# A transform and MLP kernel: first batch from rows in natural order, copies within SBUF, weight chunks interleaved with the first steps

## The chip, the cores and the metric

One core of one Trainium2 chip. The time is device microseconds of one execution; medians of several runs are given. A profile shows the clock as 1.00 wherever the trace has no record of it; there the spacing of the matmul passes has to be read instead. Ratios are the mean time of one kernel's runs over that of the other's of the same rounds, so not quite the ratio of the medians that are quoted.

## The reference

A 2-D Fourier transform (real part) over 8 batches of 3008 x 256, and on its result an MLP with a sigmoid-approximated GELU, 256 to 2048 to 256. The two weights reach the core as 64-bit floats.

```python
X = np.fft.fft(x, axis=1)              # x: (8, 3008, 256)
X = np.fft.fft(X, axis=2)
y = X.real.astype(np.float32).reshape(24064, 256)
h = y @ w_in                           # (256, 2048)
g = h * (1.0 / (1.0 + np.exp(-1.702 * h)))
out = (g @ w_out).astype(np.float32)   # (2048, 256)
```

## The kernel before

The transform over 3008 = 94 x 32 rows is done in two stages. Stage 1 needs row m together with the row that mirrors it, so x is copied once in reversed order through DRAM (`turn`), loaded beside itself, folded in place on VectorE and GpSimd (`fold1`), and multiplied (`mix1`). A spill to DRAM and a fill from it (`spill`, `fill`) turn the result to the layout of stage 2. The last transform, over 256, is folded into w_in (`fold_w`). SBUF is the core's on-chip memory; PSUM is the small one beside it into which TensorE writes its sums. The main loop has 384 steps, 48 a batch; one step makes 256 hidden columns twice (`hidden`), a GELU, four sums of the fast product (`sums`) and 28 matmul passes into the output (`product`). `pa` and `pb` are the results of `hidden`, `psa` those of `nyquist_weights`, four columns for each chunk of w_in.

Both weights come in four chunks each, and each chunk is rounded from 64 to 32 bits: a square on ScalarE and a clamp on GpSimd (`bounds`), five operations on VectorE and an integer add on GpSimd (`rounded`).

```python
def rounded(out, key):
    ...
    dve.scalar_tensor_tensor(m[:], g[:], LOW * LOW, m[:], op0=ALU.is_ge, op1=ALU.mult)
    dve.tensor_scalar(r, lo, scalar1=28, scalar2=1, ...)
    dve.tensor_scalar(a[:], bits, ...)
    dve.scalar_tensor_tensor(a[:], bits, 0xC0000000, a[:], ...)
    dve.scalar_tensor_tensor(a[:], lo, 29, a[:], ...)
    nc.gpsimd.tensor_tensor(out.bitcast(U32), a[:], r, op=ALU.add)
def sums(t):                                # per step
    nc.gpsimd.tensor_tensor(s1, a21, a22, op=ALU.add)
    nc.gpsimd.tensor_tensor(s3, a11, a21, op=ALU.subtract)
    nc.vector.tensor_tensor(s2, s1, a11, op=ALU.subtract)
    nc.vector.tensor_tensor(s4, a12, s2, op=ALU.subtract)
# order of the start (cut)
turn(0, 17, 32); load_x(0, ...); ...; round_in(0)
for c in range(NCH):
    fold1(0, c, ...); mix1(0, c)
load_in(3, nc.sync); spill(0); fill(0); fold_w(0)
for n in range(1, NCK):                     # all of w_in before step 0
    round_in(n); ...; fold_w(n)
nyquist_weights(); round_out(0); ...
rotate(0); stage2(0, 0, 0); stage2(0, 0, 1); nyquist(0, 0)
for i in range(1, NCK):                     # w_out in steps 0, 2, 4
    at(2 * i - 2, round_out, i)
```

## Time and profile before

The marks that matter are the end of stage 1 of the first batch, the start of step 0 (its first `pa` pass), and the start of step 7, from which TensorE works with hardly a gap.

| before | us |
|---|---|
| median of 3 runs | 2132.07 |
| end of stage 1, batch 0 | 47.2 |
| step 0 starts | 86.7 |
| step 7 starts | 149.6 |
| steps 0 to 7 | 62.9 |

Read the marks from the timeline: the first line that writes `pa` is step 0, and each further group of four `pa` passes is one step more. These are the lines of step 0 and step 7 (start, duration, engine, line):

```profile
86.72 2.07 PE L304 MATMUL pa<-pq,wcs 128*128 128x256 f32 x4
...
149.57 1.03 PE L304 MATMUL pa<-pq,wcs 128*128 128x256 f32 x4
```

### The profile page before, as it was taken

Reading aid. Unit: us, or ns where it says so; the run is one execution under the profiler, and the core shown is the slowest. Engines: PE = TensorE matmul, PEld = TensorE weight load, DVE = VectorE, ACT = ScalarE, POOL = GpSimd, SP = SyncE. Lnnn points to the kernel's source line nnn. Section 1 sums busy time; section 2 is a strip of 40 time slices with the busy share of each in tenths; the row PEclk is TensorE's granted clock in tenths of the full one; section 3 lists DMA queues with packets and bytes.
Section 4 is the critical chain, followed back from the end, with each engine's and each line's share of the span. In section 5 each row is a group of like instructions: output and inputs, shape, how many; then the busy total and the mean of one; then the engine's idle time right before and its main releaser. Section 6 shows DMA issues by size and latency. Waiting matters only on the chain.

```text
span 2130.6 us, 36175 instructions
## 1 busy us (share of the span) xinstructions
PE 2030.1 (95%) x14594; PEld 1907.7 (90%) x14594; DVE 1427.3 (67%) x2713; ACT 674.1 (32%) x947; POOL 772.0 (36%) x1061
## 2 busy tenths in 40 slices
PE   4579999999999999999999999999999999999998
PEld 2379999999999999998999899999999999999997
DVE  4466666766676667666666766676666667667666
ACT  1223333333333333333333333333333333333332
POOL 3445322353224522254223432244322542222222
PEclk9779999999999999999999999999999999999999
DMA  7701151123321034211421124121332112101100
GB/s 213 204 20 6 50 112 6 47 25 65 78 40 19 20 65 81 50 6 50 84 35 47 18 42 109 6 49 23 65 79 25 6 45 50 17 20 11 20 21 20
DMA packets 44098, 103.87 MB, mean 49 GB/s; under 512 B 4770, under 2 KB 29090, under 8 KB 41566
## 3 DMA queue, kind: packets, MB, share of 16 engines
q1 hardware_dynamic: 42848, 97.29, 24.4%
q10 hardware_dynamic: 1084, 4.29, 0.6%
q8 instruction: 114, 1.87, 0.4%
q14 instruction: 52, 0.43, 0.1%
HBM read 58.31 MB, written 48.78 MB: 50 GB/s over the span
## 4 chain that ended last, share of the span: by engine, by line
PE 41%; DVE 38%; issue 11%; ACT 7%; DMA 2%; POOL 1%; ACTq 0%; DVEq 0%; SPq 0%; POOLq 0%
PE po L351 24%; DVE dif L316 8%; DVE h L311 7%; DVE h L318 7%; PE pa L304 6%; DVE s L335 6%; PE pb L304 6%; DVE s L336 6%; ACT v L310 5%; PE ps L179 2%; DVE u L374 1%; PE ps L208 1%; DVE os L374 1%; ACT xt L185 1%; DMA Xr<-in_x_dram 1%
## 5 line engine op out<-in xcount | busy, mean ns | idle before, releaser
L323 ACT ACTIVATE h<-h 128x1024 f32<-128x1024 f32 x384 | 405.9, 1057 | 1370.1 <-DVE h L318 1346.2
L333 POOL TENSOR_TENSOR s<-h 128x256 f32<-128x256 f32 x384 | 279.8, 729 | 1260.3 <-issue 931.1
L351 PE MATMUL po<-wt,s 128*128 128x128 f32 x4608 | 650.3, 278 | 25.7 <-DVE s L335 25.7
L311 DVE TENSOR_TENSOR h<-v,pb 128x512 f32<-128x512 f32 x384 | 264.0, 687 | 607.5 <-ACT v L310 581.0
L351 PEld LDWEIGHTS po<-wt,s 128*128 128x128 f32 x4608 | 585.9, 194 | 26.5 <-DVE s L335 26.5
L351 PE MATMUL po<-wo,h 128*128 128x128 f32 x3072 | 474.4, 277 | 24.7 <-DVE u L374 23.5
L351 PEld LDWEIGHTS po<-wo,h 128*128 128x128 f32 x3072 | 433.5, 193 | 56.9 <-DVE u L374 38.7
L304 PE MATMUL pa<-pq,wcs 128*128 128x256 f32 x1536 | 397.5, 381 | 0.0
L304 PE MATMUL pb<-pq,wcs 128*128 128x256 f32 x1536 | 395.1, 380 | 0.0
L316 DVE SCALAR_TENSOR_TENSOR dif<-nb,af,pb 128x256 f32<-128x256 f32 x768 | 332.0, 473 | 0.0
L304 PEld LDWEIGHTS pb<-pq,wcs 128*128 128x128 f32 x1536 | 292.4, 190 | 40.0
L304 PEld LDWEIGHTS pa<-pq,wcs 128*128 128x128 f32 x1536 | 267.3, 192 | 25.2 <-issue 1.5
L318 DVE TENSOR_TENSOR h<-v,dif 128x512 f32<-128x512 f32 x384 | 275.0, 716 | 13.2
L334 POOL TENSOR_TENSOR s<-h 128x256 f32<-128x256 f32 x384 | 280.1, 729 | 0.0
L335 DVE TENSOR_TENSOR s<-s,h 128x256 f32<-128x256 f32 x384 | 247.5, 645 | 20.8 <-POOL s L333 20.8
L351 PE MATMUL po<-wo,s 128*128 128x128 f32 x1536 | 236.4, 277 | 0.0
L351 PE MATMUL po<-wt,h 128*128 128x128 f32 x1536 | 235.7, 276 | 0.0
L310 ACT COPY v<-pa 128x512 f32<-128x512 f32 x384 | 219.6, 572 | 2.6 <-PE pa L304 2.6
L336 DVE TENSOR_TENSOR s<-h,s 128x256 f32<-128x256 f32 x384 | 202.6, 528 | 13.1
L351 PEld LDWEIGHTS po<-wo,s 128*128 128x128 f32 x1536 | 204.6, 194 | 0.0
L351 PEld LDWEIGHTS po<-wt,h 128*128 128x128 f32 x1536 | 203.9, 193 | 0.0
L167 POOL TENSOR_TENSOR xt<-xt 94x510 f32<-94x510 f32 (+1 forms) x59 | 78.3, 1327 | 4.6
(57 smaller groups left out, 715.7 us busy)
## 6 DMA issues: line engine op xcount, KB each, us to landing
out_dram<-os SPq DMA_DIRECT2D x176, 128.0 KB
Td<-xt SPq DMA_DIRECT2D x8, 1536.0 KB
t<-Td SPq DMA_DIRECT2D x8, 1536.0 KB
Xr<-in_x_dram SPq DMA_DIRECT2D x8, 1410.0 KB
xt<-in_x_dram SPq DMA_DIRECT2D x7, 1280.0 KB
xt<-Xr SPq DMA_DIRECT2D x7, 1200.0 KB
nb<-pq SPq DMA_DIRECT2D x23, 256.0 KB
raw<-in_moe_w_out_dram SPq DMA_DIRECT2D x4, 1024.0 KB
```

The lines of the kernel that those rows point to most:

```text
L167: eng.tensor_tensor(low, low, free(t, up + D - 1, [-D, n], [-1, D - 1]), op=ALU.add)
L304: nc.tensor.matmul(ps[:, i * 256:(i + 1) * 256], lhsT=wcs[cs][:, f * 128:(f + 1) * 128], rhs=pq[:, cs, ks], start=True, stop=True)
L310: nc.scalar.copy(v[:], pa[:])
L311: nc.vector.tensor_tensor(h[:, 0].rearrange("p f k -> p (f k)"), v[:], pb[:], op=ALU.add)
L316: nc.vector.scalar_tensor_tensor(dif[:, c], nb[:, ks], af2[:, f:f + 1], pb[:, c], op0=ALU.mult, op1=ALU.subtract)
L318: nc.vector.tensor_tensor(free(h[:], 512 + NB - 1, [NB, 16], [-1, NB]), v[:].rearrange("p (a k) -> p a k", k=NB), dif[:].rearrange("p (a k ...
L323: nc.scalar.activation(ht[t][:], ht[t][:], ACTF.Gelu_apprx_sigmoid)
L333: nc.gpsimd.tensor_tensor(s1, a21, a22, op=ALU.add)
L334: nc.gpsimd.tensor_tensor(s3, a11, a21, op=ALU.subtract)
L335: nc.vector.tensor_tensor(s2, s1, a11, op=ALU.subtract)
L336: nc.vector.tensor_tensor(s4, a12, s2, op=ALU.subtract)
L351: nc.tensor.matmul(pot[n][:, i, q, :], lhsT=lhs[:, q * 128:(q + 1) * 128], rhs=rhs, start=(p == 0 and i == 0 and q == 0), stop=(p == NP - ...
```

## The change

Its intent is to start the main loop earlier. The first batch is no longer reversed: stage 1 takes rows in natural order with extra matrices (`w1x`) for the mirrored rows, so x is loaded straight in four chunks, at the price of twice the matmuls. Its result is moved to the layout of stage 2 by twelve copies within SBUF. Only the first chunk of w_in and of w_out is made before step 0; the others are spread over steps 0 to 5, and GpSimd's last part of a rounding (`finish_...`) is put behind the next step's sums.

```diff
+    def mix_first(c): ...
+                nc.tensor.matmul(ps[...], lhsT=w1[:, l0, :], rhs=el[:, q, c0:c1], start=True, stop=False)
+                nc.tensor.matmul(ps[...], lhsT=upper, rhs=eu[:, 3 - q, c0:c1], start=False, stop=True)
+    def shuffle_first():
+        t4 = t4t[0] = tp.tile([128, NG, D], F32, tag="t4", name="t4")
+        for a in range(NG):
+            nc.sync.dma_start(out=t4[:, a, :], in_=xt[0][8 * a:8 * a + 8, 0:16, :])
...
-        nc.gpsimd.tensor_tensor(out.bitcast(U32), a[:], r, op=ALU.add)
+        return lambda: nc.gpsimd.tensor_tensor(out.bitcast(U32), a[:], bits, op=ALU.add)
...
-    turn(0, 17, 32)
-    load_x(0, [(0, 8), (8, 16)])
+    load_first()
...
+    shuffle_first()
     bounds(("in", 0))
     bounds(("in", 1))
     round_in(0)
+    finish_in(0)
+    load_in(2, nc.sync)
+    fold_w(0)
...
+    at(0, round_in, 2)
+    at(1, fold_w, 1)
+    at(1, finish_in, 2)
+    at(1, round_out, 1)
+    at(2, finish_out, 1)
+    at(2, round_in, 3)
+    at(3, fold_w, 2)
...                       # (cut: loads, bounds, rotate, chunks 2 and 3)
```

More of the change, by code (lines that the diff above doesn't have):

```diff
@@ L33 @@
 NW = 19
+NX = 15
 PIECES = (0, 80), (80, 94)
@@ L57, in tables @@
     cos, sin = np.cos(angle), np.sin(angle)
-    w1 = np.zeros((NA, NW, NG * NU, 2))
+    w1 = np.zeros((NA, NW + NX, NG * NU, 2))
     w1[:, 1:16, :, 0], w1[:, 1:16, :, 1] = cos[:, 1:16], sin[:, 1:16]
@@ L61, in tables @@
     w1[:, 17, :, 0], w1[:, 18, :, 1] = sin[:, 0], sin[:, 16]
+    w1[:, NW:, :, 0], w1[:, NW:, :, 1] = cos[:, :16:-1], -sin[:, :16:-1]
     j, k2 = np.arange(16)[:, None], np.arange(NB)[None, :]
@@ L81, in tables @@
     small = [t.reshape(128, -1) for t in (m2, rot, cd)]
-    return w1.reshape(NA, NW, 96).astype(np.float32), np.concatenate(small, 1).astype(np.float32)
+    return w1.reshape(NA, NW + NX, 96).astype(np.float32), np.concatenate(small, 1).astype(np.float32)
 @with_exitstack
@@ L185, in mix1, with load_first, fold_first, mix_first @@
         nc.scalar.copy(full[:, 2 * c:2 * c + 2, :].rearrange("p j d -> p (j d)"), ps[0:96, :])
+    e4 = {}
+    def load_first():
+        t = xt[0] = xp.tile([96, NB, D], F32, tag="x", name="xt")
+        src = x[0].rearrange("(p j) d -> p j d", j=NB)
+        for c in range(4):
+            for lo, hi in (((0, 4), (29, 32), (16, 17)), ((4, 8), (25, 29)), ((8, 12), (21, 25)), ((12, 16), (17, 21)))[c]:
+                for p0, p1 in PIECES:
+                    nc.sync.dma_start(out=t[p0:p1, lo:hi, :], in_=src[p0:p1, lo:hi, :])
+    def fold_first(c):
+        t = xt[0]
+        el, eu = (hp.tile([NA, 4, D], F32, tag="h", name=n) for n in ("el", "eu"))
+        e4[c] = el, eu
+        first = 29 - 4 * c
+        runs = [(el, 0, 4 * c, 4, False)]
+        runs += [(eu, 0, first, 4, True)] if c else [(eu, 0, first, 3, True), (eu, 3, 16, 1, False)]
+        for e, i, lo, n, flip in runs:
+            fwd, rev = free(t[0:NA], lo * D + 1, [D, n], [1, H - 1]), free(t[0:NA], lo * D + D - 1, [D, n], [-1, H - 1])
+            nc.gpsimd.tensor_copy(free(e[:], i * D, [D, n], [H, 2]), free(t[0:NA], lo * D, [D, n], [H, 2]))
+            nc.vector.tensor_tensor(e[:, i:i + n, 1:H], fwd, rev, op=ALU.add)
+            nc.vector.tensor_tensor(e[:, i:i + n, H + 1:D], *((rev, fwd) if flip else (fwd, rev)), op=ALU.subtract)
+    def mix_first(c):
+        ps = bank("ps1")
+        el, eu = e4[c // 2]
+        for i in range(2):
+            jj, o = 2 * c + i, i * D
+            q = jj % 4
+            ends = ((0, 16, 0, H + 1), (17, 18, H + 1, D)) if jj == 0 else ((jj, NW + jj - 1, 0, D),)
+            for l0, l1, c0, c1 in ends:
+                upper = w1[:, l1, :] if l1 < NW else w1x[:, l1 - NW, :]
+                nc.tensor.matmul(ps[0:96, o + c0:o + c1], lhsT=w1[:, l0, :], rhs=el[:, q, c0:c1], start=True, stop=False)
+                nc.tensor.matmul(ps[0:96, o + c0:o + c1], lhsT=upper, rhs=eu[:, 3 - q, c0:c1], start=False, stop=True)
+        nc.scalar.copy(xt[0][:, 2 * c:2 * c + 2, :].rearrange("p j d -> p (j d)"), ps[0:96, :])
+    def shuffle_first():
+        t4 = t4t[0] = tp.tile([128, NG, D], F32, tag="t4", name="t4")
+        for a in range(NG):
+            nc.sync.dma_start(out=t4[:, a, :], in_=xt[0][8 * a:8 * a + 8, 0:16, :])
     def spill(b):
@@ L193, in fill, with rotate @@
         nc.sync.dma_start(out=t4[:], in_=Td[b].rearrange("(a p) d -> p a d", p=128))
-    def rotate(b):
-        col = t4t[b][:, :, H]
+    def rotate(b, a0=0, a1=NG, copy=None):
+        col = t4t[b][:, a0:a1, H]
         ps = bank("psr")
-        nc.tensor.matmul(ps[:, 0:NG], lhsT=rot, rhs=col, start=True, stop=True)
-        nc.vector.tensor_copy(col, ps[:, 0:NG])
+        nc.tensor.matmul(ps[:, 0:a1 - a0], lhsT=rot, rhs=col, start=True, stop=True)
+        (copy or nc.vector.tensor_copy)(col, ps[:, 0:a1 - a0])
     def stage2(b, blk, cs):
@@ L252, in rounded @@
         a = cv.tile([128, 1024], U32, tag="a", name="a")
-        r = g[:].bitcast(U32)
         dve = nc.vector
         dve.scalar_tensor_tensor(m[:], g[:], LOW * LOW, m[:], op0=ALU.is_ge, op1=ALU.mult)
-        dve.tensor_scalar(r, lo, scalar1=28, scalar2=1, op0=ALU.logical_shift_right, op1=ALU.bitwise_and)
         dve.tensor_scalar(a[:], bits, scalar1=3, scalar2=0x3FFFFFF8, op0=ALU.logical_shift_left, op1=ALU.bitwise_and)
@@ L260, in rounded, with finish_in, finish_out @@
         dve.scalar_tensor_tensor(a[:], lo, 29, a[:], op0=ALU.logical_shift_right, op1=ALU.bitwise_or)
-        nc.gpsimd.tensor_tensor(out.bitcast(U32), a[:], r, op=ALU.add)
+        dve.tensor_scalar(bits, lo, scalar1=28, scalar2=1, op0=ALU.logical_shift_right, op1=ALU.bitwise_and)
+        return lambda: nc.gpsimd.tensor_tensor(out.bitcast(U32), a[:], bits, op=ALU.add)
     wst = {}
+    last = {}
     def round_in(n):
         wst[n] = hp.tile([128, 2, 512], F32, tag="h", name="wst")
-        rounded(wst[n][:].rearrange("p i f -> p (i f)"), ("in", n))
+        last["in", n] = rounded(wst[n][:].rearrange("p i f -> p (i f)"), ("in", n))
     def round_out(n):
         ps = slice(2 * n, 2 * n + 2)
-        rounded(wo[:, ps].rearrange("p f q n -> p (f q n)"), ("out", n))
+        last["out", n] = rounded(wo[:, ps].rearrange("p f q n -> p (f q n)"), ("out", n))
+    def finish_in(n):
+        last["in", n]()
+    def finish_out(n):
+        ps = slice(2 * n, 2 * n + 2)
+        last["out", n]()
         b11, b12, b21, b22 = (wo[:, ps, q, :] for q in range(4))
@@ L282, in fold_w, with nyquist_weights @@
             nc.scalar.copy(wcs[cs][:, n * 512:(n + 1) * 512], ps[:])
-    def nyquist_weights():
+    def nyquist_weights(n):
         ps = bank("psa")
-        for f in range(NF):
+        for f in range(4 * n, 4 * n + 4):
             nc.tensor.matmul(ps[:, f:f + 1], lhsT=wcs[1][0:1, f * 128:(f + 1) * 128], rhs=ones[:, 0:1],
                              start=True, stop=True)
-        nc.vector.tensor_scalar(af2[:], ps[:, 0:NF], scalar1=2.0, scalar2=None, op0=ALU.mult)
+        nc.scalar.activation(af2[:, 4 * n:4 * n + 4], ps[:, 4 * n:4 * n + 4], ACTF.Copy, scale=2.0)
     NP = NF // 2
@@ L390 @@
     NCK = DF // 512
-    turn(0, 17, 32)
-    load_x(0, [(0, 8), (8, 16)])
+    assert NCK == 4
+    w1x = tp.tile([128, NG, D], F32, tag="t4", name="w1x")[0:NA].rearrange("p a d -> p (a d)")[:, 0:NX * 96]
+    w1x = w1x.rearrange("p (j n) -> p j n", j=NX)
+    for p0, p1 in PIECES:
+        nc.scalar.dma_start(out=w1[p0:p1], in_=tab1[p0:p1, 0:NW])
+    for p0, p1 in PIECES:
+        nc.scalar.dma_start(out=w1x[p0:p1], in_=tab1[p0:p1, NW:])
+    load_first()
+    load_in(0, nc.scalar)
     nc.scalar.dma_start(out=small[:], in_=tab2)
-    load_in(0, nc.scalar)
-    for p0, p1 in PIECES:
-        nc.scalar.dma_start(out=w1[p0:p1], in_=tab1[p0:p1])
+    load_in(1, nc.scalar)
+    load_out(0, nc.scalar)
     nc.vector.memset(ones[:], 1.0)
-    for n in range(1, 3):
-        load_in(n, nc.scalar)
+    for c in range(4):
+        fold_first(c)
+        if c:
+            mix_first(2 * c - 2)
+            mix_first(2 * c - 1)
+    mix_first(6)
+    mix_first(7)
+    shuffle_first()
     bounds(("in", 0))
@@ L402 @@
     round_in(0)
-    for c in range(NCH):
-        fold1(0, c, nc.gpsimd if c in (1, 4, 6) else nc.vector)
-        mix1(0, c)
-    load_in(3, nc.sync)
-    spill(0)
-    fill(0)
-    fold_w(0)
-    bounds(("in", 2))
-    for n in range(1, NCK):
-        round_in(n)
-        load_out(n - 1, nc.sync)
-        bounds(("in", n + 2) if n + 2 < NCK else ("out", n + 2 - NCK))
-        fold_w(n)
-    nyquist_weights()
-    round_out(0)
-    load_out(3, nc.sync)
-    if B > 1:
-        turn(1, 17, 32)
-        load_x(1)
-    rotate(0)
+    finish_in(0)
+    load_in(2, nc.sync)
+    fold_w(0)
+    bounds(("out", 0))
+    round_in(1)
+    finish_in(1)
+    load_out(1, nc.sync)
+    nyquist_weights(0)
+    bounds(("in", 2))
+    round_out(0)
+    finish_out(0)
+    load_in(3, nc.sync)
+    rotate(0, 0, 4, nc.scalar.copy)
     for cs in range(2):
@@ L432 @@
     n = len(steps)
-    for i in range(1, NCK):
-        at(2 * i - 2, round_out, i)
-        if i + 1 < NCK:
-            at(2 * i - 2, bounds, ("out", i + 1))
+    at(0, round_in, 2)
+    at(0, load_out, 2, nc.sync)
+    at(0, bounds, ("out", 1))
+    at(1, fold_w, 1)
+    at(1, nyquist_weights, 1)
+    at(1, rotate, 0, 4, NG)
+    at(1, finish_in, 2)
+    at(1, round_out, 1)
+    at(1, load_out, 3, nc.sync)
+    at(1, bounds, ("in", 3))
+    if B > 1:
+        at(1, turn, 1, 17, 32)
+        at(1, load_x, 1)
+    at(2, finish_out, 1)
+    at(2, round_in, 3)
+    at(2, bounds, ("out", 2))
+    at(3, fold_w, 2)
+    at(3, nyquist_weights, 2)
+    at(3, finish_in, 3)
+    at(3, round_out, 2)
+    at(3, bounds, ("out", 3))
+    at(4, finish_out, 2)
+    at(4, round_out, 3)
+    at(5, fold_w, 3)
+    at(5, nyquist_weights, 3)
+    at(5, finish_out, 3)
     for b in range(B):
```

## The prediction

> **What bounds the kernel now.** I read the page's slices first. TensorE is at nine tenths or more from the fourth slice on (a slice is 53 us); only the first three are thin, and that is the part this change touches.
>
> ```profile
> PE   4579999999999999999999999999999999999998
> ...
> PEclk9779999999999999999999999999999999999999
> ```
>
> Then the timeline, to find where TensorE becomes the bound. The loop's steps are counted by their four `pa` passes. Step 0 begins at 86.72 us, step 7 at 149.57 us. From step 7 on one step follows another without a wait, 0.87 + 0.86 + 3.12 = 4.85 us each for the hidden pieces and the product. Whatever lies behind step 7's start is TensorE-bound and the same in both kernels, so its 2130.6 - 149.6 = 1981.0 us are taken as fixed, and the prediction is one question: when does step 7 start in the changed kernel?
>
> Third, the chain of waits over the first 160 us (start, duration, what):
>
> ```profile
> 0.74 18.29 DMA Xr<-in_x_dram
> ...
> 21.12 8.46 DMA xt<-Xr
> ...
> 41.83 5.40 PE ps L179 x12
> 47.23 4.91 PE psw L281 x8
> ...
> 55.47 9.50 DMA raw<-in_moe_w_out_dram
> ...
> 69.28 3.70 PE psw L281 x8
> 72.98 3.67 PE psa L287 x32
> ...
> 86.79 2.00 PE pa L304 x4
> ...
> 97.88 2.39 POOL wo L261
> 100.27 0.07 issue
> 100.33 0.73 POOL wt L275
> ```
>
> The reader is to see three stages: 29.6 us in which x is reversed through DRAM and loaded, about 18 us of first-stage matmuls, about 40 us in which all four chunks of w_in are rounded and folded one after another, and then steps 0 to 6 at 19.9 us for two steps (92.73 to 112.65 to 132.57 us, the starts of the rounding of w_out), because GpSimd finishes a whole chunk (2.39 + four times 0.73 + 1.06 us) before it may make the sums of the step.
>
> Last, the first-stage matmul by itself, first 60 us and then 150 us to the end (durations are minimum/median/maximum):
>
> ```profile
> L179 PE MATMUL ps<-xt,w x30: 631/634/743, 31.8 to 46.6; 94*96 94x256 f32 x30
> ...
> L179 PE MATMUL ps<-xt,w x210: 377/378/420, 160.2 to 1749.2; 94*96 94x256 f32 x105
> ```
>
> and the same stage beside the next one on TensorE:
>
> ```profile
> 37.99 9.24 PE L179 MATMUL ps<-xt,w 94*96 94x256 f32 x20 [1.20 <-DVE xt L170]
> 47.02 8.53 PE L281 MATMUL psw<-wst,small 128*128 128x512 f32 x16
> ```
>
> In the first batch a pass of 256 columns is spaced at about 0.43 us; later four passes take 0.87 us, 0.22 each. In all of its 15 us the first stage never reached the faster rate; the 128x128 fold passes after it went from 0.86 to 0.43 us at 50.2 us.
>
> **What the Trainium skill says.** "TensorE: Matmul & The Clock Gate", section "What's actually happening": two clock states, half rate when idle and full rate after about 3.4 us of sustained work. The trace has the two rates (634 against 378 ns), and full-size passes warm within 3.2 to 6 us here, but the 94x96 passes of 37.99 to 47.23 us stayed at the slow rate for over 9 us. Trace and page differ; I follow the trace. "DMA: Bandwidth & Descriptors", section "Two DMAs through the same engine are not ordered": a DMA that reads what another wrote must wait for its semaphore. The trace agrees: the fill through Td is issued at 55.00 us, 7.1 us after the spill at 47.92 us. Same page, "How many engines (k)" in the section on the semaphore's 16: the slowest dimension of both sides decides, so the new 8-partition copies would run on eight engines. No run here shows that yet.
>
> **The change part by part.**
>
> Removed: the DRAM reversal of batch 0, its in-place folding (26.96 to 44.1 us on VectorE and GpSimd), the spill and fill of batch 0, and the wait of step 0 for all four w_in chunks, 16 `psa` columns and the first w_out chunk.
>
> Added, loads. x comes in four chunks of about 0.77 MB on one queue, on the other w1 0.69 MB, w1x 0.54 MB, raw in 1.05 MB, small 0.46 MB, and two more raw chunks. The windows of before show 386 to 414 GB/s between 12 and 18 us. At an estimated 390 GB/s from 2 us on, split over two queues, chunk 0 and the weights are there by about 7 us, chunks 1, 2, 3 at about 11, 15 and 19 us. VectorE's fold is four operations of 508 columns a chunk; 510 columns took 0.69 us, so 2.8 us a chunk, 11 us in all, ready at about 7.7, 13, 17.5 and 24 us (chunks 2 and 3 also wait for buffers that the matmuls of chunks 0 and 1 free).
>
> Added, matmuls. Each pair of rows now takes four matmuls of 256 columns or their equal (before two, except for the end rows), two passes each: 8 x 8 = 64 such passes in place of 34 (the end rows counted by width). At 0.43 us they are 27.5 us, at 0.22 us 14 us. Starting at 7.7 to 9 us they end at M = 35 to 36.5 us if they stay slow: TensorE is then behind the loads at every chunk. If they warm up, the last chunk's arrival leads and M is 25 to 28 us.
>
> From M to step 0, on the path: last copy 0.65 us; then ScalarE's square, which now stands behind the eight copies, 1.1; five VectorE operations (1.26 + 0.69 + 1.26 + 1.26 + 0.69, 5.2 us as at 8.83 to 13.90 us); GpSimd add 2.4: M + 9.5. Four fold matmuls, cold again, 6.0 us as at 62.34 us: copies done M + 16.3. Four `psa` columns about 0.9, two more squares and small copies on ScalarE before the `rotate` copy: M + 18.9. Two stage-2 blocks, copies and the row broadcast: step 0 at about M + 21.6. The shuffle (12 copies of 128 KB) starts at M + 0.7, and its first four groups are needed only at M + 17, so I count it as hidden.
>
> From step 0 to step 7, the same durations walked in order on each engine: step 0's h ends at M + 25.7; round in 2 at 30.9; step 1's h at 34.2; then VectorE idles until 38.0 for the second `rotate`, which stands behind fold 1 and its copies on ScalarE; then four times a rounding of 5.15 us and a step of 3.3 us (0.69 + 2 x 0.43 + 0.69 + 0.65 + 0.43): h of step 5 at M + 73.6. Fold 3, its copies and `psa` lead to step 6 at M + 76.9, its hidden and product 4.9 us to step 7 at M + 81.7. The steps 0 to 7 thus take 60 us against 63 us before: GpSimd's long finish no longer stands before the sums, but the three w_in chunks have moved in. The gain is almost all in step 0: about 57 us in place of 86.7.
>
> Sum with M = 36: step 7 at 117.7 us in place of 149.6, 31.9 us less; span 2098.7, and the measured time lies 1.5 us over the span, so 2100. With M = 26: 2090.
>
> **Rivals.** (1) The doubled matmuls warm up. For it: the page, and they are back to back where before's had gaps. Against it: 9 us of nearly gapless passes without it. It would take 8 to 11 us more off: 2089 to 2092. I give it one in four. (2) The shuffle or the late weights become the wait. Eight source partitions feed each copy; if twelve took over 16 us, step 0 would slip by the excess. For the late chunks the load waits for a raw buffer: w_in 2 is issued at M + 7.5 and needed at M + 17; spare 5 us. It would cost 0 to 8 us: to 2108. (3) Batch 1's x is now loaded late: its reversal is issued only after the last w_out chunk, at about M + 43 us. Before, reversal to issue of the next load took 9.4 us (82.39 to 91.78), the load after it 8.5 us, so it lands by M + 65, and is needed in step 7. If it slips, step 8's fold waits and a few us are given back. (4) VectorE runs without the 3 to 4 us idle pieces that my order of copies gives: 4 us less.
>
> **Range and chances.** Three quarters at about 2100 with a spread of 5, one quarter at about 2090: 2098, eight times in ten within 2087 to 2108. Two per cent is 42.6 us or 2089.4; only the warm case with nothing lost elsewhere passes it, 0.17. Slower by 2% would need every part to fail: 0.01.
>
> **What would show it.** Right: step 0 at 55 to 59 us and step 7 at 115 to 120 us; the first-stage passes at a median near 634 ns from 8 to 36 us; TensorE idle for about 9 us after them; VectorE without waits over 2 us between steps 2 and 5; 4.85 us steps after step 7. Wrong: first-stage passes at 378 ns, M below 30 us, or a wait for the shuffle or for batch 1's x, or a stretch behind step 7 that isn't 1981 us.

## More of the kernel before

One line more is needed later: VectorE's first sum during the weight stage, from the listing of that source line between 60 and 155 us (durations are minimum/median/maximum in ns).

```profile
L335 DVE TENSOR_TENSOR s<-s,h x7: 655/664/929, 105.0 to 153.8; 128x256 f32<-128x256 f32 x7
```

The reader is to see that this operation takes about 0.66 us here.

## The result, and the profile after

The changed kernel takes 2134.35 us (median of 4 runs, 2132.13 to 2135.22) against 2131.74 us of before in the same rounds: ratio 1.0011, 95% interval 0.9994 to 1.0028. It is the same. The profiled run has a span of 2130.3 us; it is the fastest of the four (2132.13 us).

| mark, us | before | predicted | after |
|---|---|---|---|
| end of stage 1, batch 0 | 47.2 | 36 | 41.1 |
| step 0 starts | 86.7 | 57.6 | 73.0 |
| steps 0 to 7 | 62.9 | 60.1 | 80.3 |
| step 7 starts | 149.6 | 117.7 | 153.3 |
| from step 7 to the end of the span | 1981.0 | 1981.0 | 1977.0 |

The lines of step 0 and step 7 in the changed kernel:

```profile
72.97 2.08 PE L356 MATMUL pa<-pq,wcs 128*128 128x256 f32 x4
...
153.26 1.03 PE L356 MATMUL pa<-pq,wcs 128*128 128x256 f32 x4
```

So the loop does start 13.7 us earlier, and then the same seven steps take 17.4 us longer. The slices of the page show both: the first two are a tenth fuller than before (5 and 6 for 4 and 5), the third is a tenth emptier (6 for 7), and from the fourth on they are full as before.

```profile
PE   5669999999999999999999999999999999999998
...
PEclk9789999999999999999999999999999999999999
```

The chain of waits of the changed kernel over the first 165 us (start, duration, what) shows where the time goes. L230 is a copy within SBUF, L387 VectorE's first sum, L375 the GELU.

```profile
41.71 0.77 SPq L230
...
56.89 1.73 SPq L230
...
58.80 8.12 DMA raw<-in_moe_w_in_dram
...
70.97 2.07 PE psn L265 x2
73.04 2.00 PE pa L356 x4
...
85.64 2.19 DVE s L387
...
90.65 1.06 ACT h L375
91.71 0.97 ACT wcs L334 x2
92.67 0.04 issue
92.72 1.86 PE psa L339 x8
```

The reader is to see two things. First, issuing the twelve copies lasts from 41.7 to 58.6 us; the load of w_in chunk 2 stands behind them in the same queue, is issued at 58.8 us and read only from 67 us on, and step 0 stands behind that: not because it needs chunk 2, but because in ScalarE's order the square of chunk 2 (`bounds`) stands before the copy of `rotate`, which stage 2 of the first block waits for. Second, in the steps the chain runs over VectorE (its roundings, and first sums of up to 2.19 us) and over GELU, weight copies and `psa` in turn. What the sums meet is seen in the timeline (start, duration, engine, line; these are lines of step 5):

```profile
136.88 0.68 DVE L363 TENSOR_TENSOR h<-v,pb 128x512 f32<-128x512 f32 x1
137.04 2.36 POOL L305 TENSOR_TENSOR wo<-a,m 128x1024 uint32<-128x1024 uint32 x1 [3.02 <-DVE m L304]
137.48 2.21 DVE L387 TENSOR_TENSOR s<-s,h 128x256 f32<-128x256 f32 x1
```

VectorE's sum starts 0.44 us after GpSimd's finishing add and ends 0.3 us after it. While GpSimd works, it stands. The operation just before it, which takes one of its inputs from PSUM, keeps its 0.68 us. It started first, but the same operation of step 4 (126.91 us) runs wholly inside another finishing add (125.26 to 127.63 us) and takes 0.69 us: it is not held. The same listing as shown for before, 60 to 155 us, gives for the changed kernel:

```profile
L387 DVE TENSOR_TENSOR s<-s,h x6: 419/2213/2258, 85.6 to 150.8; 128x256 f32<-128x256 f32 x6
```

The median is 2.2 us where it was 0.66. The Trainium skill has the rule that I did not look up: "SBUF — State Buffer", section "SBUF: two separate sides", says that VectorE with two SBUF inputs and a GpSimd operation that reads SBUF share a pair of ports, that whichever starts first holds it for its whole instruction, and that the other waits. The trace agrees, as these lines show.

How much this is can be added up from one window of the steps, first before, then changed (its start and end and its length, then the busy time of TensorE's matmuls and weight loads, VectorE, ScalarE and GpSimd with the number of instructions, then clock, share of the DMA engines and GB/s):

```profile
86.72:149.57 62.85, 38.24 (x198) 35.46 (x197) 34.65 (x51) 13.76 (x17) 26.59 (x30) 0.72 0.36 95
```
```profile
72.97:153.26 80.29, 53.18 (x248) 42.63 (x247) 60.86 (x66) 19.56 (x28) 42.09 (x34) 0.75 0.37 101
```

In the changed kernel VectorE is busy for 60.9 us. Its work there is five roundings of 5.05 us (1.22 + 0.69 + 1.23 + 1.22 + 0.69), seven times 2.25 us for h (0.69 + 0.87 + 0.69), six times 0.85 us of sums (0.42 + 0.43) and 0.17 us: 46.3 us with every duration as it is when nothing else runs. Some 14.6 us are standing still inside an instruction, which the busy time hides. About half of it is in four of the six first sums; the rest is in second sums, roundings (the third operation takes 1.63 us in place of 1.23 each time) and h. In before's window, three roundings and what of h and the sums falls into it make 34.0 us so, and VectorE is busy for 34.7 us: hardly any excess, because there GpSimd's finish always stood between VectorE's work and never beside it.

The first stage has such a block too, on the last fold of x beside GpSimd's two clamps:

```profile
31.76 2.90 DVE L212 TENSOR_TENSOR eu<-xt 94x508 f32<-94x508 f32 x1
...
31.94 2.17 POOL L290 TENSOR_SCALAR m<-raw 128x1024 f32<-128x1024 f32 x2
```

The other operations of this kind there take 0.68 us; here TensorE waits 0.58 us for it.

The copies within SBUF, by windows of 2 us (first two of the first load stage, then one amid the copies, then one of a weight load alone; the last three numbers are the granted clock, the mean busy share of the 16 DMA engines and GB/s):

```profile
8.00:10.00 2.00, 0.74 (x2) 0.40 (x2) 1.04 (x2) 0.00 (x0) 0.49 (x1) 1.00 0.97 221
10.00:12.00 2.00, 0.00 (x0) 0.00 (x0) 0.33 (x1) 0.00 (x0) 0.30 (x1) 1.00 0.98 224
...
52.00:54.00 2.00, 2.00 (x4) 0.68 (x3) 1.99 (x1) 0.00 (x0) 0.91 (x1) 1.00 0.40 97
...
68.00:70.00 2.00, 1.78 (x8) 1.78 (x8) 0.00 (x0) 0.65 (x3) 2.00 (x2) 0.50 1.02 412
```

The copies move 97 GB/s and leave more than half of the engines idle (0.40), which fits the eight engines that the prediction took from the Trainium skill ("DMA: Bandwidth & Descriptors"). And the first loads move 221 to 224 GB/s with all engines busy, where a weight load alone reaches 412. This is how the first fold waits, and TensorE for it:

```profile
11.67 0.55 DVE L211 TENSOR_TENSOR eu<-xt 94x381 f32<-94x381 f32 x1 [2.63 <-DMA xt<-in_x_dram]
...
13.04 0.72 PE L224 MATMUL ps<-eu,w 94*96 94x129 f32 x2 [3.74 <-DVE eu L211]
```

In the trace the loads of the start share eight semaphores, so that from the ninth issue on (7.29 us) each waits until an earlier load has landed. But the two transfers that the first of these lines needs were issued at 1.69 and 2.05 us, without such a wait, and landed only at 10.8 and 11.6 us. The waiting of issues did not hold the first fold; the slow transfers did.

### The profile page after: what moved, and what is told of

It is laid out like the page before. It is cut to its first block, busy times and chain, and to the rows that moved or that the text cites. A ratio compares the mean times of both kernels' runs of the same rounds, so it can differ in the third digit from the quotient of the medians.

```text
span 2130.3 us, 36302 instructions
## 1 busy us (share of the span) xinstructions
PE 2039.4 (96%) x14626; PEld 1912.7 (90%) x14626; DVE 1438.3 (68%) x2707; ACT 673.6 (32%) x952; POOL 774.7 (36%) x1058
## 4 chain that ended last, share of the span: by engine, by line
DVE 43%; PE 33%; issue 12%; ACT 9%; DMA 2%; SPq 1%; ACTq 0%; DVEq 0%; POOL 0%
PE po L403 19%; DVE dif L368 10%; DVE h L363 8%; DVE h L370 8%; DVE s L387 7%; DVE s L388 7%; ACT v L362 6%; PE pa L356 5%; PE pb L356 5%; DVE u L426 1%; PE ps L181 1%; DVE os L426 1%; ACT xt L187 1%; PE ps L253 1%; ACT pq L255 1%
## 5 line engine op out<-in xcount | busy, mean ns | idle before, releaser
L375 ACT ACTIVATE h<-h 128x1024 f32<-128x1024 f32 x384 | 405.9, 1057 | 1369.6 <-DVE h L370 1345.4
L387 DVE TENSOR_TENSOR s<-s,h 128x256 f32<-128x256 f32 x384 | 250.8, 653 | 2.0 <-POOL s L385 2.0
L169 POOL TENSOR_TENSOR xt<-xt 94x510 f32<-94x510 f32 (+1 forms) x56 | 73.8, 1318 | 4.4
```

The costliest lines, as they stand in the source:

```text
L169: eng.tensor_tensor(low, low, free(t, up + D - 1, [-D, n], [-1, D - 1]), op=ALU.add)
L375: nc.scalar.activation(ht[t][:], ht[t][:], ACTF.Gelu_apprx_sigmoid)
```

## The experiments

My theory after the result: the expected gain went three ways, (a) the copies hold back a load that step 0 needs, (b) in the steps VectorE and GpSimd block each other and ScalarE's order makes VectorE wait, (c) stage 1 ends 5 us late because its loads are slow. The main rival: the interleaving is harmless, and the new first batch with its late loads is what slows everything behind it. Thirteen kernels ran, in rounds of three against before; "after" stands for the changed kernel.

| run | median us | ratio to before | step 0 | steps 0 to 7 | step 7 |
|---|---|---|---|---|---|
| after | 2134.35 | 1.0011 | 73.0 | 80.3 | 153.3 |
| e1_oldw | 2136.90 | 1.0034 | 93.4 | 60.4 | 153.8 |
| e2_oldx | 2126.64 | 0.9979 | 68.7 | 78.9 | 147.7 |
| e3_dram | 2123.69 | 0.9962 | 63.5 | 80.6 | 144.1 |
| e4_early | 2124.07 | 0.9962 | 62.8 | 80.6 | 143.5 |
| e5_noadd | 2123.65 | 0.9967 | 73.7 | 69.7 | 143.3 |
| e6_warm | 2133.96 | 1.0011 | 74.2 | 81.3 | 155.6 |
| e7_fold | 2122.60 | 0.9961 | 74.3 | 69.7 | 144.0 |
| e8_both | 2115.29 | 0.9925 | 64.4 | 68.7 | 133.0 |
| e9_all3 | 2105.82 | 0.9874 | 65.4 | 59.6 | 125.1 |
| e10_early | 2114.01 | 0.9916 | 58.4 | 75.4 | 133.8 |
| e11_pitch | 2133.97 | 1.0006 | 72.9 | 81.4 | 154.3 |
| e12_ports | 2132.09 | 1.0001 | 71.7 | 80.1 | 151.8 |
| e13_early_noadd | 2102.27 | 0.9861 | 56.0 | 67.2 | 123.2 |

The half-widths of the 95% intervals are about 0.0015 to 0.0018. No ratio differs from 1 by 2%; what is read here are smaller differences that lie outside the intervals, and the marks in the traces. Not all runs were taken in the same rounds.

**e1_oldw**: the new first batch alone.

```diff
+    for n in range(1, NCK):
+        round_in(n); finish_in(n); ...; fold_w(n)      # before step 0, as in the kernel before
-    at(0, round_in, 2) ... at(5, finish_out, 3)
+    at(2 * i - 2, round_out, i); at(2 * i - 2, finish_out, i)
```

> Only the new first batch; all weights rounded and folded before step 0, as in the kernel before. If the interleaved weights give the gain back, this is faster than the changed kernel: first stage ends near 41 us as there, then about 40 us of weights and 63 us of steps 0 to 7 as before, so step 7 near 144 us and about 2127 us. If the new first batch is itself what gives it back, step 7 stays at 150 us or later and the time at 2132 us or more.

Measured: 2136.90 us, neither of the two in full. The steps take 60.4 us, so without interleaving they are as short as before; that half held. But step 0 comes at 93.4 us and not near 81: its chain of waits goes through the same twelve copies, issued from 41.7 to 58.8 us, and through a w_in load behind them that is landed at 67.7 us. The copies hurt this order more, since here step 0 does need all four chunks of w_in and the last of them stands behind the copies. The new first batch alone makes step 0 6.7 us later than before (93.4 against 86.7). Against the changed kernel, interleaving brought step 0 forward by 20.4 us and lengthened the steps by 19.9 us.

**e2_oldx**: the interleaved weights alone, first batch as before.

```diff
-    load_first(); ... fold_first(c); mix_first(...); shuffle_first()
+    turn(0, 17, 32); load_x(0, ...); fold1(0, c, ...); mix1(0, c); spill(0); fill(0)
```

> Only the interleaved weights; first batch by the reversal through DRAM as before. If the interleaved steps are slow by themselves (80 us from step 0 to step 7, as in the changed kernel), step 0 comes near 65 us and step 7 near 145 us: about 2128 us. If the slow steps come from the new first batch and its late loads, steps 0 to 7 take 60 to 63 us: about 2110 us.

Measured: 2126.64 us, steps 78.9 us. The interleaved steps are slow without the new first batch and its loads. The main rival falls. And step 0 comes at 68.7 us, 4.3 us earlier than with the new first batch: with the copies in front of the load, the new first batch lost time at step 0.

**e3_dram** and **e4_early**: the copies replaced by a spill and fill; and the w_in load issued after four of the copies.

```diff
-    shuffle_first()
+    spill(0)                    # e3_dram
+    fill(0)
```
```diff
-    shuffle_first()
+    shuffle_first(0, 4)         # e4_early
     ...
     load_in(2, nc.sync)
+    shuffle_first(4, NG)
```

> The changed kernel with the twelve copies within SBUF replaced by one spill and one fill through DRAM. If the copies hold up the load of w_in chunk 2, that load lands near 56 instead of 67 us, step 0 comes about 10 us earlier (63 us) and the time is about 2122 us. If step 0 waits for something else (bandwidth, ScalarE's order), it stays within 2 us of 73 us and the time at 2132 us.

> The changed kernel with the load of w_in chunk 2 issued after four of the twelve copies. If only its place in the queue behind the copies costs, step 0 comes near 63 us and the time near 2122 us, as with the copies through DRAM. If the copies slow the load by sharing the DMA engines, it lands late all the same and step 0 gains under 4 us.

Measured: step 0 at 63.5 and 62.8 us, 2123.69 and 2124.07 us: both as expected. The issue line and the square that reads the load, in e4's timeline:

```profile
47.63 0.64 SPq L275 DMA_DIRECT2D raw<-in_moe_w_in_dram  x1
...
58.67 1.17 ACT L291 ACTIVATE g<-raw 128x1024 f32<-128x1024 f32 x1
```

Nothing waits in front of the second line any more. The place in the queue was the cost, 10 us, and not the copies' own landing or the shared engines: in e4 eight of the twelve are still under way when step 0's path runs. Against e2 (68.7 us) the new first batch now does bring step 0 forward, by 5 to 6 us. Part (a) is shown.

**e5_noadd**: GpSimd's finishing adds taken away; the results are truncated, a tiny error made on purpose (the result still counts as correct).

```diff
-        dve.scalar_tensor_tensor(a[:], lo, 29, a[:], ...)
+        dve.scalar_tensor_tensor(out.bitcast(U32), lo, 29, a[:], ...)
-        return lambda: nc.gpsimd.tensor_tensor(out.bitcast(U32), a[:], bits, op=ALU.add)
+        return lambda: None
```

> The changed kernel without GpSimd's eight finishing adds: the last VectorE operation of a rounding writes the result, so it is truncated and not rounded to nearest (a deliberate, tiny error). If VectorE's two-input operations stand still while GpSimd works, the sums that took 2.2 us fall to about 0.65 us, steps 0 to 7 shrink from 80 to 66 to 70 us and the time to about 2118 us (some 2 to 4 us of it from the shorter chain ahead of step 0). If the order of ScalarE's work sets the steps, the sums get shorter but the steps hardly, and the time is about 2128 us.

Measured: 2123.65 us, steps 69.7 us. The sum's listing, 60 to 155 us:

```profile
L387 DVE TENSOR_TENSOR s<-s,h x8: 410/435/954, 86.1 to 151.0; 128x256 f32<-128x256 f32 x8
```

From 2.21 to 0.44 us: the add was what it stood for. The steps shrank by 10.6 us as the first theory has it. The 2 to 4 us ahead of step 0 did not come, since step 0 waits for the load there. The run alone cannot part the collisions from the shorter chain of a rounding; the traces do. Between step 0 and step 7 VectorE's busy time fell from 60.9 to 51.2 us, with the same work, while its waits there hardly changed (14.1 and 13.5 us): what went was the standing still. Some 5 us over its 46.3 us of work remain, beside GpSimd's clamps and its own sums.

**e7_fold**: the fold of a w_in chunk one step earlier in the order.

```diff
-    at(1, fold_w, 1)
-    at(1, nyquist_weights, 1)
+    at(0, fold_w, 1)            # and chunk 2 at 2 in place of 3, chunk 3 at 4 in place of 5
+    at(0, nyquist_weights, 1)
```

> The changed kernel with the fold of w_in chunks 1, 2, 3 one step earlier in the order (after steps 0, 2, 4 in place of 1, 3, 5), so that its copies on ScalarE no longer wait for the next step's GELU. If the chain GELU, copies, psa, hidden, VectorE sets the steps, VectorE's idle pieces of 4.6, 1.7 and 7.9 us go, steps 0 to 7 take about 66 us and the time is about 2118 us. If VectorE against GpSimd is what sets them, at most 4 us come off: 2128 us or more.

Measured: 2122.60 us, steps 69.7 us. VectorE's waits between step 0 and step 7 (us in total, times, longest), first in the changed kernel, then in e7:

```profile
DVE h L363 <- PE pb L356: 22.8, 3, 13.3
DVE t L245 <- PE psr L244: 4.6, 1, 4.6
```
```profile
DVE h L363 <- PE pb L356: 18.2, 4, 13.9
```

The longest is the one before step 0. Without it 14.1 us became 4.3 us, and the steps lost 10.6 us; VectorE's busy time stayed (60.9 and 60.2 us). So ScalarE's order costs as much as the collisions, and this, too, I had expected a little larger (14 us).

**e6_warm**: five full-size matmuls on constants in the middle of stage 1.

```diff
+        if c == 2:
+            for i in range(5):
+                nc.tensor.matmul(ps[:], lhsT=dummy[:, 0:128], rhs=dummy[:], ...)
```

> The changed kernel with five full-size 128x512 matmuls on constant data between the first-stage matmuls of chunks 0 and 1. If the clock, once it is up, stays up under 94x96 passes, the passes after them fall from 634 to 378 ns, the first stage ends near 38 us (then bound by the arrival of the last chunk) and the time falls by about 3 us. If the shape itself keeps or brings the slow rate, the passes stay at 634 ns, the first stage ends near 47 us and the time rises by about 6 us.

Measured: 2133.96 us. The clock rose about 1 us into those 5 us (the first full-size pass is spaced at 0.85 us, the second at 0.53, the others at 0.43) and stayed up under the 94x96 passes that followed:

```profile
18.62 1.06 PE L224 MATMUL ps<-eu,w1x 94*96 94x256 f32 x2
19.47 4.98 PE L463 MATMUL warm<-dummy 128*128 128x512 f32 x10
24.29 0.60 PE L223 MATMUL ps<-el,w 94*96 94x256 f32 x2
...
31.20 0.59 PE L223 MATMUL ps<-el,w 94*96 94x256 f32 x2
36.19 1.14 PE L224 MATMUL ps<-eu,w1x 94*96 94x256 f32 x2 [4.39 <-DVE eu L212]
```

Two passes take 0.60 us where they took 1.06, until TensorE waits 4.4 us for the last chunk and is slow again. The end of stage 1 did not move to 38 us but to 42.4: with a fast TensorE the last chunk's load and fold are the bound, and the rest then ran at the slow rate. About 2 us of the 4.4 are again VectorE's last fold beside GpSimd's clamps, 2.88 us in place of 0.68. Inconclusive for the time, clear for the clock.

**e8_both** (e4 and e7) and **e9_all3** (e4, e5 and e7): the edits are those shown.

> Both repairs: w_in chunk 2 loaded after four copies, and the folds one step earlier. If the two waits are separate, the gains add: step 0 near 63 us, steps 0 to 7 near 66 us, about 2110 us. If the earlier step 0 only moves the wait into the late w_out loads, the steps stay at 80 us and the time at about 2123 us.

> Both repairs and also no finishing adds on GpSimd (results truncated, a deliberate tiny error). With VectorE's collisions and ScalarE's order both gone the prediction's own walk should hold: steps 0 to 7 in 58 to 62 us, time near 2107 us. If the steps stay at 66 us or more, a third cause is in them.

Measured: e8 2115.29 us; by the marks both gains are there in full (step 0 at 64.4, steps 68.7 us), though 5 us above the 2110 hoped for, since e7's own share had been put at 14 us and was 10.6. e9 2105.82 us, steps 59.6 us. With the finishing adds and the order gone, the steps take what the prediction's walk said, 60.1 us. That the two agree so closely is in part luck: the walk has the adds, which e9 lacks, and in e9 VectorE is still busy for 51.0 us, some 5 us more than its work, which the walk lacks. No third cause of size is needed for the steps. Part (b) is shown.

**e10_early** and **e13_early_noadd**: e8 with the squares of w_in ahead of the last fold, chunk 0 rounded under stage 1 and chunk 2 before step 0; and the same without the finishing adds.

```diff
+        if c == 3:
+            bounds(("in", 0)); bounds(("in", 1))
         fold_first(c)
...
+    round_in(0)                 # ahead of the last two mix_first
+    round_in(2)                 # ahead of step 0; later roundings move up by one step
```

> An attempt to beat both: e8 with the squares of w_in chunks 0 and 1 ahead of the last fold, the rounding of chunk 0 while TensorE still does the first stage, chunk 2 loaded and rounded before step 0, and one rounding fewer inside the steps. If VectorE's idle time under the first stage can be used, step 0 comes near 54 to 58 us, steps 0 to 7 take 60 to 64 us and the time is about 2096 us. If the copies within SBUF then set step 0, it stays at 60 us or later and the time is above 2102 us.

> e10 without the finishing adds on GpSimd (truncated results, a deliberate tiny error). If e10 gained little because VectorE and GpSimd block each other, this gains at least as much over e10 as e9 gained over e8 (9 us): 2105 us or less, with step 0 near 55 us. If VectorE is simply full of its own work there, it stays above 2108 us.

Measured: e10 2114.01 us. Step 0 came to 58.4 us as hoped, and the steps grew to 75.4 us: step 7 starts at 133.8 us, in e8 at 133.0. Work was moved, not saved, and the time is 18 us above the 2096 hoped for. e13 2102.27 us, a ratio 0.0055 below e10's, no less than e9 gained over e8 (0.0051): with the adds gone the same early order pays. VectorE and GpSimd block each other there; VectorE by itself is not yet full (busy for 44.3 of the 67.2 us of e13's steps).

**e11_pitch** and **e12_ports**: why the first loads are slow. x read from contiguous 4 KB pieces; and as many bytes written to 128 partitions in place of 94. Their outputs are wrong, which doesn't matter for the times.

```diff
-   dma_start(out=t[p0:p1, lo:hi, :], in_=src[p0:p1, lo:hi, :])
+   dma_start(out=t[p0:p1, lo:hi, :], in_=flat[2 * c + (lo > 15)][p0:p1, 0:hi - lo, :])      # e11
+   dma_start(out=t[p0:p1, lo * D:lo * D + n], in_=view(x[0], ..., [n, p1 - p0], [1, n]))    # e12: 80 + 48 partitions
```

> The changed kernel with the first batch's x read from contiguous 4 KB pieces in place of pieces 32 KB apart (the wrong rows, so a wrong result on purpose). If the spacing in DRAM is what keeps the loads of the first 30 us at 190 to 290 GB/s, they rise to about 390 GB/s, the first fold ends near 9 us in place of 13, the last chunk lands near 22 us in place of 31, and the first stage, on TensorE alone, ends near 37 us: 4 us less. If the cut into small transfers with eight in flight is what limits them, the landings and the time stay as they are.

> The changed kernel with the same bytes of x, in as many transfers, spread over 128 partitions in place of 94 (wrong places, so a wrong result on purpose; the unwritten rest is filled with a constant). If the number of partitions written limits the loads, they rise above 330 GB/s, the last chunk lands near 25 us in place of 31 and the first stage ends 2 to 4 us earlier. If the many small transfers with eight in flight limit them, rate and landings stay.

Measured: neither. In e11 the windows stay at 187 to 320 GB/s and the first fold ends at 12.8 us; in e12 at 193 to 334 GB/s, with the first fold complete at 10.7 us in place of 13.1, the last chunk's second fold starting at 28.9 us in place of 31.2 and stage 1 ending 2.2 us earlier. Spacing in DRAM is excluded. The spread over partitions is worth some 2 us of the 5 at most; it cannot be told from the cut into pieces, as each second piece of e12 covers 48 partitions in place of 14, and the times of e12 and of the changed kernel are not told apart (ratios 1.0001 and 1.0011). That many small transfers with eight in flight are the limit is what is left of the two causes I named; but for the first fold the eight are not it, as the transfers that it waited for were issued at once (see above; in e12 the same two landed at 8.7 and 9.2 us). Why they are slow no run shows, and it stays open.

## Why the prediction was wrong

The prediction said 2098 us, 2087 to 2108; measured was 2134.35. By its own sum the error is 35.6 us at the start of step 7 (153.3 in place of 117.7), and it splits by the marks.

- **Stage 1's rate: right.** Its passes stayed at the slow rate throughout, from 13.0 to 41.1 us with one gap of 0.58 us, 28 us against 27.5 worked out. The rival of a warm clock was rightly held to be less likely.
- **"At an estimated 390 GB/s from 2 us on": wrong, 5.1 us.** The rate was taken from windows in which whole weight chunks were moving. The first fold was complete at 13.1 us and not at 7.7; the whole stage shifted by that. Why the first transfers were that slow stays open (e11, e12).
- **"I count it as hidden" (the shuffle): wrong, 10.3 us.** The groups that step 0 needs did not hold it. What I missed is that twelve issues take 16.9 us of the queue and that `load_in(2)` stands behind all of them: issued 17.7 us after stage 1, not 7.5. The second rival named both halves, "if twelve took over 16 us" and the late weights, but not that the one stands in the other's queue, and priced them at 0 to 8 us with no run for it; e3 and e4 give 9 to 10 us.
- **The walk from step 0 to step 7: wrong, 20.2 us, the largest term.** It took "the same durations walked in order on each engine", from a kernel in which GpSimd's finish and VectorE's sums never met. Laid beside each other they block: the first sums mostly took 2.2 us in place of 0.65, and 14.6 us of standing still are counted as busy; taking the adds away gives 10.6 us back (e5). The rest is ScalarE's order: the walk names one wait of VectorE, 3.8 us before the second `rotate`, and it waited 14.1; rival 4, that even this wait goes, went the other way. Putting the folds earlier gives 10.6 us back (e7). A sum of the walk is also not what it says: 38.0 and four times 5.15 + 3.3 us make M + 71.8, not M + 73.6; the 1.8 us are not explained. The collisions were read as a gain ("GpSimd's long finish no longer stands before the sums"). e9, without the adds and with the folds earlier, needs 59.6 us.
- **The fixed rest, 1981.0 us:** it was 1977.0, 4 us less. This is why the span came out equal although step 7 starts 3.7 us later. Some small waits of TensorE in the later loop differ: 1.3 us of it is there by step 11, the rest comes piecemeal. It goes with the interleaving: e1 has 1980.5 us, every run with interleaved weights 1976.2 to 1978.4. Why was not followed.
- **Rival 3, batch 1's x too late:** its reversal was issued at 101.7 us, later than thought, but the fold of step 7 starts at 155.8 us without a wait. Right that it costs nothing.

So where did the expected gain go? The new first batch did end stage 1 6.1 us earlier, but its copies then cost step 0 more than that (e1 and e2). The interleaving brought the loop's start forward, 13.7 us net. But the roundings that left the start went into the steps, where GpSimd's part of them stands in VectorE's way and where the folds' copies wait behind the GELU: 17.4 us back.

A version that beats both with exact rounding is e10 (2114.01 us, ratio 0.9916), with e8 1.3 us behind it by the medians, which the intervals do not tell apart; with truncated weights e13 (2102.27 us, 0.9861).

## What to carry to other kernels

When work is moved to run beside other work, take its durations from a place where both run together, or ask which port, queue or order they share; a busy engine may be standing still inside its instruction. A group of cheap transfers can cost its issue time to whatever stands behind it in the same queue, so put the load that the next stage needs in front. And when a move brings one mark forward, look at once at how long the stretch behind it became: e1, the changed kernel and e10 differ by up to 35 us at step 0, while e1 and the changed kernel start step 7 within 0.6 us of each other.

## What the Trainium skill lacked or had wrong

- "TensorE: Matmul & The Clock Gate", section "What's actually happening": some 3.4 us of sustained work bring the full rate. Here 94x96 passes ran for 28 us with one gap of 0.58 us (1.06 us for two) and never reached it; in e6, after 6 us of them, 128x128 passes with 512 columns reached it in about 1 us, and the same 94x96 passes then held it for 7 us (0.60 us for two). The section does not say that the size of what is multiplied matters for the rise; whether it is the rows, the columns or the length of the pass is not told apart here.
- "SBUF — State Buffer", section "SBUF: two separate sides": right, and it would have corrected the prediction. A 0.42 us sum took 2.21 us beside a 2.36 us GpSimd add. What it lacks is that the profile counts the wait as busy time.
- "DMA: Bandwidth & Descriptors": the rule for the number of engines fits the copies of 8 partitions (busy share 0.40 of 16 engines). The page has no figure for such copies; here twelve of 128 KB took 16.9 us to issue and moved 97 GB/s (52 to 54 us).
- Same page: no rate for many smaller transfers in flight together. Loads of x (14 to 320 KB each) and of the stage-1 matrices ran at 187 to 337 GB/s in windows with all engines busy, while a 1 MB weight load reached 412; DRAM spacing (e11) does not explain it, and the spread over partitions (e12) at most 2 us of 5.
